# Layer norm, SwiGLU forward and value projection as one written stage; SwiGLU backward in written order; all activations turned by DMA transposes

## The chip, the cores and the metric

One core of one Trainium2 chip. The metric is the device time of one execution in microseconds (us). Each kernel was run several times beside the kernel before on the same chip; all runs that enter a ratio are of the same (fast) state. Most readings below are of stages, because two executions of the same code differ by 10 us and more in the long middle of this program, whatever was changed at its ends (4327 to 4366 us in the fifteen profiles with the change).

Names: PE is TensorE, DVE VectorE, ACT ScalarE, Pool GpSimd and SP SyncE; a DMA queue is called after the engine that issues its transfers. PSUM tiles are the buffers that the matmuls write to. The clock is the share of PE's full clock that was granted, the DMA share the mean busy share of the 16 DMA engines. A turned load is a DMA issued with `dma_start_transpose`: it transposes what it moves (the trace has it as DMA_TRANSPOSE; where the recorded texts say crossbar, they mean these). A hole is a stretch in which PE stands idle.

## The reference, cut to what matters

```python
xn = _layernorm(x)                         # x: 2048 x 640, bf16
s  = recurrent_attention(xn, mem0, Wq, Wk, Wv, Wo)   # 64 segments of 32 rows, 32 heads of 128
h  = silu(xn @ w1) * (xn @ w3)             # 2048 x 1728
g  = silu(h @ w2)                          # 2048 x 640
out = x + s * g
# returned: out, and the gradients of x, mem0, Wq, Wk, Wv, Wo, w1, w3, w2 (jax.vjp)
```

The scans over the segments, forward and backward, are the long middle. The change rewrites what lies in front of them (layer norm, SwiGLU forward, projections of the first rows) and behind them (gradient of Wo, SwiGLU backward, gradients of w1, w3, w2). Some small loads in the scans change their form.

Of the kernel before, what the change touches and what calls it, by code (L numbers as in the profile page):

```python
# [16 lines left out]
P = 128  # L17
# [23 lines left out]
class K:  # L41
# [55 lines left out]
    def setup_consts(self):  # L97
# [9 lines left out]
        self.mean_all = const.tile([P, self.NT], F32, name="mean_all")  # L107
# [44 lines left out]
    def setup_dram(self):  # L152
# [7 lines left out]
        self.XNT = mk("XNT", (D, S))  # L160
        self.SLT = mk("SLT", (F, S))
        self.DUT = mk("DUT", (F, S))
        self.HB = mk("HB", (S, F))
# [3 lines left out]
        self.GST = mk("GST", (D, S))  # L167
# [191 lines left out]

def phase3_Afwd(k, W4, Wv, Wk_):  # L360
# [5 lines left out]
    with tc.tile_pool(name="b0", bufs=1) as io, tc.tile_pool(name="b0s", bufs=3) as stp, \  # L366
            tc.tile_pool(name="b0p", bufs=4, space=bass.MemoryType.PSUM) as ps:
        xs = io.tile([P, DC, k.NB0], BF16, name="b0x")
        nc.sync.dma_start(xs[:], k.XNT[:, 0:k.NB0].rearrange("(dc p) t -> p dc t", p=P))
        wq = k.A_Wq.rearrange("(dc p) h e -> p dc (h e)", p=P)  # L370
        wo = k.A_Wo.rearrange("h e d -> e h d")
        fetch = [(Wq[:, dc], wq[:, dc]) for dc in range(DC)] + [(Wo[:, h:h + 8], wo[:, h:h + 8]) for h in range(0, H, 8)]
        n = 0
        for wi, (W, dst) in enumerate(((Wv, k.QVX[:, 1]), (Wk_, k.KX[:, :]), (Wq, k.QVX[:, 0]))):
            for x0 in range(0, k.NB0, 112):
                for cg in range(4):
                    if n % 3 == 0 and n > 5 and fetch:
                        nc.scalar.dma_start(*fetch.pop(0))
                    n += 1
                    st = stp.tile([112, 1024], BF16, name="b0st", tag="b0st")  # L380
                    for b in range(2):
                        c0 = cg * 1024 + b * 512
                        pb = ps.tile([112, 512], F32, name="b0pb", tag="b0pb")
                        for dc in range(DC):
                            nc.tensor.matmul(pb[:], xs[:, dc, x0:x0 + 112], W[:, dc, c0:c0 + 512],
                                             start=(dc == 0), stop=(dc == DC - 1))
                        k.copy(st[:, b * 512:(b + 1) * 512], pb[:], eng='vs'[b])
                    nc.sync.dma_start(dst[x0:x0 + 112, cg * 1024:(cg + 1) * 1024], st[:])
        assert not fetch

    with tc.tile_pool(name="ast", bufs=1) as st, tc.tile_pool(name="achain", bufs=1) as ch, \
# [22 lines left out]
        def ride_ld(t):  # L414
            x0 = k.NB0 + 24 * t
            b, sub = t // 4, t % 4
            if sub == 0 and x0 < S:
                w = min(96, S - x0)
                rt = ch.tile([P, DC, 96], BF16, name="ride", tag="ride")
                nc.sync.dma_start(rt[:, :, 0:w], k.XNT[:, x0:x0 + w].rearrange("(dc p) s -> p dc s", p=P))  # L420
# [340 lines left out]
def gx_ld(k, xs, x0, eng):  # L761
    w = min(P, k.S - x0)
    eng.dma_start(xs[:, :, 0:w], k.GST[:, x0:x0 + w].rearrange("(dc p) t -> p dc t", p=P))
# [13 lines left out]
def phase3b_out(k, Wo, W0, W4):  # L777
# [12 lines left out]
    with tc.tile_pool(name="oio", bufs=1) as io, tc.tile_pool(name="oac", bufs=1, space=bass.MemoryType.PSUM) as pa, \  # L790
# [59 lines left out]
        def gox_ld(x0):  # L850
            xs = io.tile([P, DC, P], BF16, name="g0x", tag="g0x", bufs=2)
            gx_ld(k, xs, x0, nc.scalar)
# [60 lines left out]
def phase4_Abwd(k, out2, WoT, WvT, WkT, WqT, later):  # L913
# [3 lines left out]
    with tc.tile_pool(name="gst", bufs=1) as st, tc.tile_pool(name="gchain", bufs=1) as ch, \  # L917
# [26 lines left out]
        def ride_ld(t):  # L944
# [3 lines left out]
            if sub == 3:  # L948
                rt = ch.tile([P, DC, 96], BF16, name="gride", tag="gride")
                nc.sync.dma_start(rt[:], k.GST[:, 96 * b:96 * b + 96].rearrange("(dc p) s -> p dc s", p=P))  # L950
# [279 lines left out]
        def gox(x0, cg, b):  # L1230
            if cg == 0 and b == 0:
                uu["gx"] = ch.tile([P, DC, P], BF16, name="gx0", tag="xp", bufs=1)
                gx_ld(k, uu["gx"], x0, nc.gpsimd)
# [263 lines left out]
def phase6b_gWo(k, gow, orr0, out6, gz, late):  # L1497
# [4 lines left out]
    with tc.tile_pool(name="o6", bufs=1) as hp, tc.tile_pool(name="o6i", bufs=2) as io, \  # L1502
# [28 lines left out]
        for qd in range(8):  # L1531
            orr = orrs[qd]
            for jp in range(2):
# [4 lines left out]
                if qd > 1 and late:  # L1538
                    out_, in_ = late.pop(0)
                    if in_ is k.w2:  # L1540
                        turned_load(k, out_, in_)
                    else:
                        nc.scalar.dma_start(out_, in_)
# [8 lines left out]
                for j in range(2):  # L1552
# [4 lines left out]
                    nc.sync.dma_start(out6f[hh * P:(hh + 1) * P, :], ot[:])  # L1557
# [5 lines left out]
def phase1_ln(k: K):  # L1563
    nc, tc = k.nc, k.tc
    D, DC, NT = k.D, k.DC, k.NT
    with tc.tile_pool(name="ln_io", bufs=3) as io, tc.tile_pool(name="ln_sm", bufs=4) as sm, \
            tc.tile_pool(name="ln_ps", bufs=2, space=bass.MemoryType.PSUM) as ps:
        half = D // 2
        assert half <= nc.vector.BN_STATS_FMAX
        for tt in range(NT):  # L1570
            xt = io.tile([P, D], BF16, name="xt", tag="xt")
            k.dma(xt[:], k.A_x[tt * P:(tt + 1) * P, :])
            stats = sm.tile([P, 2, nc.vector.BN_STATS_DIM], F32, name="stats", tag="stats")
            xv = xt[:].rearrange("p (a b) -> p a b", a=2)
            nc.vector.bn_stats(stats[:, 0, :], xv[:, 0, :])
            nc.vector.bn_stats(stats[:, 1, :], xv[:, 1, :])
            mv = sm.tile([P, nc.vector.BN_AGGR_DIM], F32, name="mv", tag="mv")
            nc.vector.bn_aggr(mv[:], stats[:])
            rs = k.rstd_all[:, tt:tt + 1]
            nc.scalar.activation(rs, mv[:, 1:2], ACT.Sqrt, bias=k.eps_t[:], scale=1.0)  # L1580
            nc.vector.reciprocal(rs, rs)
            nc.vector.tensor_copy(k.mean_all[:, tt:tt + 1], mv[:, 0:1])
            nmr = sm.tile([P, 1], F32, name="nmr", tag="nmr")
            nc.vector.tensor_tensor(nmr[:], mv[:, 0:1], rs, ALU.mult)
            nc.vector.tensor_scalar(nmr[:], nmr[:], -1.0, None, op0=ALU.mult)
            xn = io.tile([P, D], BF16, name="xn_t", tag="xn_t")
            nc.vector.tensor_scalar(xn[:], xt[:], rs, nmr[:], op0=ALU.mult, op1=ALU.add)
            k.dma(k.XN[tt * P:(tt + 1) * P, :], xn[:])
            pt = ps.tile([P, DC, P], BF16, name="lnT", tag="lnT")
            for dc in range(DC):  # L1590
                nc.tensor.transpose(pt[:, dc, :], xn[:, dc * P:(dc + 1) * P], k.ident[:])
            xnT = io.tile([P, DC, P], BF16, name="xnT_t", tag="xnT_t")
            k.copy(xnT[:], pt[:])
            k.dma(k.XNT[:, tt * P:(tt + 1) * P].rearrange("(dc p) t -> p dc t", p=P), xnT[:])



def phase2_Bfwd(k: K, Wv, Wk_):
    nc, tc = k.nc, k.tc
    D, DC, S, F, FC = k.D, k.DC, k.S, k.F, k.FC  # L1600
    BLK = 512
    NBLK = S // BLK
    fszs = [min(P, F - fc * P) for fc in range(FC)]
    with tc.tile_pool(name="bw", bufs=1) as wp, tc.tile_pool(name="bio", bufs=2) as io, \
            tc.tile_pool(name="bwork", bufs=2) as wk, \
            tc.tile_pool(name="bps", bufs=2, space=bass.MemoryType.PSUM) as ps, \
            tc.tile_pool(name="bps1", bufs=1, space=bass.MemoryType.PSUM) as ps1:
        w1s = wp.tile([P, DC, F], BF16, name="w1s")
        k.dma(w1s[:], k.w1.rearrange("(dc p) f -> p dc f", p=P))
        w3s = wp.tile([P, DC, F], BF16, name="w3s")  # L1610
        k.dma(w3s[:], k.w3.rearrange("(dc p) f -> p dc f", p=P))
        w2s = wp.tile([P, FC, D], BF16, name="w2s")
        for fc in range(FC):
            k.dma(w2s[:fszs[fc], fc, :], k.w2[fc * P:fc * P + fszs[fc], :])

        nc.gpsimd.dma_start(Wv[:], k.A_Wv.rearrange("(dc p) h e -> p dc (h e)", p=P))
        k.x_rows(k.HRO, k.XN, nc.gpsimd)
        for blk in range(NBLK):
            if blk == 1:
                nc.gpsimd.dma_start(Wk_[:], k.A_Wk.rearrange("(dc p) h e -> p dc (h e)", p=P))  # L1620
            b0 = blk * BLK
            xnT = io.tile([P, DC, BLK], BF16, name="xnT_b", tag="xnT_b")
            nc.scalar.dma_start(xnT[:], k.XNT[:, b0:b0 + BLK].rearrange("(dc p) t -> p dc t", p=P))
            hBT = io.tile([P, FC, BLK], BF16, name="hBT", tag="hBT")
            for fc in range(FC):
                fsz = fszs[fc]
                pg = ps.tile([P, BLK], F32, name="pg", tag="pg")
                pu = ps.tile([P, BLK], F32, name="pu", tag="pu")
                for dc in range(DC):
                    nc.tensor.matmul(pg[:fsz, :], w1s[:, dc, fc * P:fc * P + fsz], xnT[:, dc, :],  # L1630
                                     start=(dc == 0), stop=(dc == DC - 1))
                for dc in range(DC):
                    nc.tensor.matmul(pu[:fsz, :], w3s[:, dc, fc * P:fc * P + fsz], xnT[:, dc, :],
                                     start=(dc == 0), stop=(dc == DC - 1))
                sig = wk.tile([P, BLK], BF16, name="sig", tag="sig")
                nc.scalar.activation(sig[:fsz], pg[:fsz], ACT.Sigmoid)
                sl = wk.tile([P, BLK], BF16, name="sl", tag="sl")
                nc.vector.tensor_tensor(sl[:fsz], pg[:fsz], sig[:fsz], ALU.mult)
                ut = wk.tile([P, BLK], BF16, name="ut", tag="ut")
                nc.scalar.copy(ut[:fsz], pu[:fsz])  # L1640
                nc.vector.tensor_tensor(hBT[:fsz, fc, :], sl[:fsz], ut[:fsz], ALU.mult)

                ds = wk.tile([P, BLK], BF16, name="ds", tag="ds")
                nc.vector.scalar_tensor_tensor(ds[:fsz], sig[:fsz], 1.0, sl[:fsz], op0=ALU.subtract, op1=ALU.mult)
                nc.vector.tensor_tensor(ds[:fsz], sig[:fsz], ds[:fsz], ALU.subtract)
                nc.vector.tensor_tensor(ds[:fsz], ds[:fsz], ut[:fsz], ALU.mult)
# [264 lines left out]
```

## The kernel before: the parts that the change touches

Layer norm is a phase of its own and writes its rows (XN) and their transposes (XNT). Then SwiGLU forward, in blocks of 512 rows, with a scheduler free to order it:

```python
nc.gpsimd.dma_start(Wv[:], ...)                     # 5.2 MB
k.x_rows(k.HRO, k.XN, nc.gpsimd)                    # rows into the scans' layout, DRAM to DRAM, 2.5 MB
for blk in range(4):
    xnT <- XNT (plain load, scalar)
    for fc in range(14):                            # hidden chunks of 128 (the last: 64 rows)
        pg, pu = 5 + 5 matmuls of 512 columns       # w1, w3
        sig (ACT), sl, hBT, ds x3 (DVE), stores of sl and ds on sync
    for ti in range(4):
        pz = 28 matmuls of 320 columns (w2); gb, dz, gs (DVE) and their stores
        5 transposes of gs and 14 of hBT by matmuls with the identity, copied by DVE and ACT
    # ... (cut)
```

SwiGLU backward at the end, in blocks of 256 rows:

```python
for b0 in range(0, S, 256):
    xn_all[...] <- XN                               # gpsimd
    for f0 in range(0, 14, 2):                      # pairs of hidden chunks
        sl, du <- SLT, DUT                          # scalar, three buffers
        pghb = 5 matmuls; ggT = pghb * du; guT = pghb * sl      # DVE
    for ti in range(2):
        pgx = 56 matmuls of 320 columns             # row gradient
        28 transposes of ggT, guT by matmuls, copied by DVE and ACT; store of gu
        norm of the row gradient, o1 = ... (gpsimd), store
```

## Time and profile before

| | us |
|---|---|
| time before, median of 3 runs | 5483.78 (5476.4 to 5496.66) |
| first hidden matmul | 61.7 |
| projections of the first rows over | 492.1 |
| scans and their gradients, to the first matmul of the gradient of Wo | 4339.6 |
| gradient of Wo, of w2 | 175.7, 85.2 |
| SwiGLU backward loop (first hidden matmul to first matmul of the gradient of w1) | 258 |
| gradients of w1, w3 | 117 |

The windows of these stages, from the profile of the kernel before (length, busy time with counts of PE, PE's weight loads, DVE, ACT, POOL; then granted clock, DMA share, GB/s):

```profile
62.00:330.00 268.00, 225.53 (x1313) 116.75 (x1311) 176.28 (x360) 99.78 (x161) 3.12 (x4) 0.92 0.55 189
330.00:492.00 162.00, 159.31 (x720) 94.98 (x720) 49.67 (x72) 41.54 (x71) 0.00 (x0) 0.98 0.49 161
...
5094.00:5352.00 258.00, 238.79 (x1904) 163.36 (x1905) 144.89 (x353) 42.36 (x64) 26.63 (x23) 0.99 0.39 118
```

The projections are full of matmuls; the stage in front of them loses 42 us and some clock; the loop is busy for 239 of 258 us at a clock of 0.99, but 448 of its 1904 matmuls are transposes. Read the DMA share beside them: 0.39 in the loop looks like room.

### The profile page before, as it was taken

What the parts mean: (1) busy time and instruction counts of PE and PEld (TensorE: products, weight loads), DVE (VectorE), ACT (ScalarE), POOL (GpSimd) and SP (SyncE); (2) the same over time, 40 slices, a digit from 0 to 9 for tenths busy, and PEclk for the clock granted to TensorE, in tenths of its full rate; (3) what the DMA queues carried; (4) which work ended last, traced back from release to release, by engine and by line L of the source; (5) the groups of instructions that cost most, each with busy time, mean ns of one, the idle gap of its engine ahead of it and who ended that gap; (6) DMA issues with size and microseconds to landing.
All of it is one profiled execution on the core that took longest, in us unless ns stands there. A gap on an engine that the chain in (4) does not pass through costs nothing. (4 is left out here: it accounts for less than half of the span.)

```text
span 5474.2 us, 163087 instructions
## 1 busy us (share of the span) xinstructions
PE 4830.6 (88%) x66012; PEld 3050.2 (56%) x66012; DVE 2297.2 (42%) x7285; ACT 1752.0 (32%) x4913; POOL 1558.4 (28%) x2673
## 2 busy tenths in 40 slices
PE   4988899989999785999999998789998999999999
PEld 2544555555555443555666665555566555666665
DVE  5833555555555423444444443322233222311451
ACT  2422455555555422232333332222233222301111
POOL 0000334343444212333333332432344333310100
PEclk9998999999999787999999999899999999999999
DMA  7553455555544587666766664744355444657332
GB/s 248 177 188 91 134 154 159 154 159 156 159 154 149 131 190 156 175 185 173 194 182 179 185 184 111 164 113 96 96 134 124 111 106 97 167 178 184 111 111 94
DMA packets 1004358, 822.92 MB, mean 150 GB/s; under 512 B 507009, under 2 KB 892333, under 8 KB 1000929
## 3 DMA queue, kind: packets, MB, share of 16 engines
q1 hardware_dynamic: 758779, 559.22, 37.2%
q0 software_dynamic: 95696, 155.10, 10.3%
q10 hardware_dynamic: 149130, 98.17, 6.5%
q8 instruction: 521, 8.54, 0.7%
q14 instruction: 232, 1.90, 0.1%
HBM read 476.95 MB, written 303.09 MB: 142 GB/s over the span
## 5 line engine op out<-in xcount | busy, mean ns | idle before, releaser
L1411 PE MATMUL wg<-gr,hr 128*128 128x512 bf16 x2400 | 529.4, 382 | 16.1 <-DVE dST L1335 12.9
L1390 PE MATMUL g<-w,ghacc 128*128 128x320 bf16 x3072 | 456.8, 307 | 0.0
L1411 PEld LDWEIGHTS <-hr 128*128 128x128 bf16 x2400 | 235.5, 98 | 301.5 <-issue 27.3
L1390 PEld LDWEIGHTS <-ghacc 128*128 128x128 bf16 x3072 | 301.9, 100 | 120.1
L308 PEld LDWEIGHTS <-hx 128*32 128x32 bf16 x7680 | 180.0, 97 | 170.0 <-issue 13.7
L90 DVE CAST wgo<-wg 128x512 bf16<-128x512 f32 x72 | 47.5, 687 | 524.5 <-issue 268.1
L90 DVE CAST stg<-bank 128x512 bf16<-128x512 f32 x256 | 177.0, 691 | 208.9 <-PE bank L308 197.2
L327 PEld LDWEIGHTS <-gkv 128*8 128x8 bf16 x8192 | 189.8, 87 | 109.1 <-DVE gkv L1002 24.6
L611 ACT ACTIVATE xP<-xsp,xnm 120x120 bf16<-120x120 f32 (+1 forms) x704 | 240.0, 375 | 8.7 <-DVE xnm L607 5.4
L660 POOL DMA_DIRECT2D OR<-xv x163 | 92.7, 569 | 470.5 <-ACT xv L659 347.7
L1154 POOL DMA_DIRECT2D DSR<-gdS x176 | 101.0, 574 | 434.7 <-DVE gdS L1152 410.7
L92 ACT CAST wgo<-wg 128x512 bf16<-128x512 f32 x48 | 25.8, 589 | 572.0 <-PE wg L1411 572.0
L1351 ACT CAST gr<-r6p 120x512 bf16<-120x512 f32 x160 | 93.8, 586 | 357.5 <-PE r6p L1344 255.3
L1223 PE MATMUL gbank<-WqT,ident 128*128 128x512 bf16 x640 | 204.8, 404 | 0.0
L622 POOL TENSOR_TENSOR xP<-xP,xrz 120x480 bf16<-120x480 bf16 x163 | 161.7, 992 | 136.1 <-ACT xP L611 96.1
L1399 DVE TENSOR_TENSOR ghacc<-ghacc,g 128x320 f32<-128x320 f32 x192 | 93.5, 487 | 244.7 <-PE g L1390 244.7
L1152 DVE SCALAR_TENSOR_TENSOR gdS<-gdp,Dx,gPr 120x120 bf16<-120x120 f32 (+1 forms) x680 | 182.8, 330 | 0.0
L245 POOL DMA_DIRECT2D r<-GOS x256 | 144.0, 566 | 130.1 <-PE r6p L1344 92.1
L1359 POOL DMA_DIRECT2D GSP<-grs x48 | 25.6, 539 | 534.6 <-ACT grs L1351 517.4
L308 PE MATMUL gbank<-WoT,gox 128*32 128x512 bf16 x2560 | 153.6, 386 | 24.2 <-POOL gox L957 20.9
L327 PE MATMUL bank<-Wo,oTm 128*32 128x320 bf16 x4032 | 170.2, 320 | 0.1
L1123 POOL DMA_DIRECT2D VTD<-gvT x176 | 130.6, 744 | 137.1 <-ACT gvT L1122 115.8
(342 smaller groups left out, 11150.4 us busy)
## 6 DMA issues: line engine op xcount, KB each, us to landing
QVS<-stg SPq DMA_DIRECT2D x128, 256.0 KB
gqv<-QVS SPq DMA_DIRECT2D x108, 192.0 KB
vTt<-VTD SPq DMA_DIRECT2D x64, 320.0 KB
VTD<-gvT POOLq DMA_DIRECT2D x168, 120.0 KB, 3.6
DSR<-gdS POOLq DMA_DIRECT2D x168, 120.0 KB, 3.5
dS<-DSR SPq DMA_DIRECT2D x168, 120.0 KB
P<-PR SPq DMA_DIRECT2D x168, 120.0 KB
gPr<-PR SPq DMA_DIRECT2D x164, 120.0 KB
```

The lines of the kernel that those rows point to most:

```text
L90: return nc.vector.tensor_copy(out, in_)
L245: eng.dma_start(d, src if src.shape[0] > 1 else src[0])
L308: k.nc.tensor.matmul(bank[32 * g:32 * g + 32, :], x[:, dc, :], W[:, dc, c0:c0 + 512], start=(dc == 0), stop=(dc == k.DC - 1), tile_positio ...
L327: k.nc.tensor.matmul(pm[p0:p0 + nq, 0:320], x[:, h, :], W[:, h, 320 * b:320 * b + 320], start=(first and i == 0), stop=(last and i == 15), ...
L611: nc.scalar.activation(Pb[0:n, j, 0:n], sp[0:n, j, :], ACT.Exp, bias=nmx[0:n, j:j + 1], scale=k.scale, accum_out=Z[0:n, j:j + 1])
L622: eng.tensor_tensor(Pb[0:n, :, 0:n], Pb[0:n, :, 0:n], bc_last(rz[0:n], n), ALU.mult)
L1123: nc.gpsimd.dma_start(k.VTD[tl][:, :, h0:h0 + 4, :], vTq[:])
L1152: nc.vector.scalar_tensor_tensor(dS[0:n, j, 0:n], dp[0:n, j, :], Dx[0:n, j:j + 1], Pr[0:n, j, 0:n], op0=ALU.subtract, op1=ALU.mult)
L1154: nc.gpsimd.dma_start(k.DSR[tl][:, h0:h0 + 4, :], dS[0:n])
L1223: nc.tensor.matmul((bA if g in ("W1", "G1", "G2") else bB)[:], k.ident[:], WqT[:, 0, 0:512], start=True, stop=True)
L1390: nc.tensor.matmul(pg[:], ring[:, i, j, r0:r0 + P], Ws[qd][i][:, j, 320 * h:320 * h + 320], start=(i == 0 and j == 0), stop=(i == 2 and j ...
L1411: nc.tensor.matmul(accs[dc][:], hr[:, tl, dc * P:(dc + 1) * P], grs[i][:, tl, :], start=(tl == 0), stop=(tl == NF - 1))
```

## The change

Its intent: take the transposes off TensorE and let turned loads bring everything that must be turned; start the hidden matmuls early by joining layer norm with SwiGLU forward; put the down projection of a block between the hidden chunks of the next; in the backward loop put the row gradient of a block between the hidden products of the next, so that PE never waits for DVE. Both stages are fixed to their written order on every engine. The core of the diff, with cuts:

```diff
-            nc.gpsimd.dma_start(Wv[:], ...); k.x_rows(k.HRO, k.XN, nc.gpsimd)
+    for blk in range(NBLK):
+        for fc in range(FC):
+            hidden(blk, fc)                      # stores of sl and ds on gpsimd now
+            if blk == 0:  ...                    # layer norm of the later tiles, spread over fc
+                if fc == 9:  fetch(1)            # turned load of the next block's rows (SP)
+                if fc == 12: nc.scalar.dma_start(Wv[:], ...)
+                if fc == 13: k.x_rows(k.HRO, k.XN, nc.sync)
+            elif fc == 0: hidden_out(blk - 1); up_ld(blk - 1, 0); up_ld(blk - 1, 1)   # Gt, scalar, 2 buffers
+            elif fc < 9 and fc % 2 == 0: up(blk - 1, fc // 2 - 1)                     # down projection
+            elif fc == 9: fetch((blk + 1) % NBLK)
+            elif fc == 11 and blk == 1: nc.scalar.dma_start(Wk_[:], ...)
+    # ... (the projection of the first rows with Wv, the last block's up between them)
-                nc.tensor.transpose(pgs..., gs...); nc.tensor.transpose(pht..., hBT...)   # gone
-            nc.sync.dma_start(rt, k.XNT[...])
+            turned_load(k, rt, k.XN[...])        # also gride and gx in the scans, from GS
@@ backward loop
+    for n, (b, i) in enumerate(pairs):
+        ld(n + 3)                                # sl on scalar, du on gpsimd, 4 buffers
+        hid(b, i)                                # products; one turned load of ggT per chunk (SP)
+        next(work, None)                         # a piece of the row gradient of block b - 1
+        if i == FC // 2 - 1:
+            hid_out(b)                           # store of gu, gpsimd, 0.88 MB
+            rows_ld(b)                           # xn_all on gpsimd; gar, ln_G on scalar
+            work = rowgrad(b)                    # calls norm: scr on ACT, o1 and its store on gpsimd
```

## The prediction

> **What bounds the kernel now.** I read the page first: PE is busy 88% of 5474.2 us, and the digits of its row dip at the very start only, so the question is what PE does there and at the end, the two places that the change rewrites. The middle (about 495 to 5007 us) keeps its written order. I then cut the first 500 us and the last 650 us into windows, asked each for its groups, and followed the end by the chain of waits. The windows of the start:
>
> ```profile
> 0.00:20.00 20.00, 0.00 (x0) 0.00 (x0) 1.73 (x9) 0.00 (x0) 3.33 (x22) 1.00 0.93 339
> 20.00:50.00 30.00, 7.63 (x55) 5.09 (x55) 22.61 (x97) 8.16 (x18) 0.00 (x0) 1.00 0.81 229
> 50.00:100.00 50.00, 25.61 (x100) 11.12 (x101) 19.96 (x61) 11.41 (x20) 3.12 (x4) 0.83 0.84 311
> ...
> 150.00:200.00 50.00, 49.84 (x307) 26.36 (x305) 40.67 (x84) 23.93 (x39) 0.00 (x0) 1.00 0.54 173
> ```
>
> The columns are length, then busy time of PE, PE's weight loads, DVE, ACT, POOL, then granted clock, DMA share, GB/s. For 20 us nothing computes while 339 GB/s of weights arrive ahead of the inputs; from 20 to 50 us the layer norm is DVE's; from 50 to 100 us PE waits half the time at a clock of 0.83. From 150 us on PE is full. The groups of the first 560 us say with what:
>
> ```profile
> L1638 DVE TENSOR_TENSOR sl<-pg,sig 128x512 bf16<-128x512 f32 (+1 forms) x56 | 38.3, 684 | 19.5 <-DMA SLT<-sl 13.8 <-ACT sig L1636 4.1 <-ACT ut L1640 0.8
> L1644 DVE SCALAR_TENSOR_TENSOR ds<-sig,sl 128x512 bf16<-128x512 bf16 (+1 forms) x56 | 38.2, 683 | 17.6 <-DMA DUT<-ds 17.5
> L1646 DVE TENSOR_TENSOR ds<-ds,ut 128x512 bf16<-128x512 bf16 (+1 forms) x56 | 23.5, 419 | 0.9
> L1682 PE MATMUL pht<-ident,hBT 128*128 128x128 bf16 x224 | 16.8, 218 | 2.1 <-ACT hb_tok L1686 2.1
> ```
>
> The SLT and DUT rows are early stalls behind stores (31 us of DVE), which PE feels; pht is a transpose by identity matmuls that the change drops. The windows of the end, then the chain of waits there:
>
> ```profile
> 4829.00:5010.00 181.00, 177.57 (x1299) 127.28 (x1300) 30.22 (x67) 12.92 (x34) 25.46 (x48) 0.99 0.73 229
> 5010.00:5040.00 30.00, 17.23 (x151) 12.38 (x149) 3.44 (x7) 4.56 (x7) 1.43 (x2) 0.85 1.08 205
> 5040.00:5100.00 60.00, 59.04 (x410) 37.48 (x408) 11.13 (x28) 5.02 (x13) 4.23 (x6) 0.99 0.18 54
> 5100.00:5350.00 250.00, 233.01 (x1857) 158.79 (x1856) 138.44 (x334) 40.85 (x61) 22.39 (x18) 0.99 0.38 116
> ```
>
> ```profile
> 4831.70 175.31 PE oa L1550 x1277
> ...
> 5017.54 17.78 DMA x<-in_B_w_dram
> ```
>
> So the gradient of Wo is a solid matmul stretch, 175.31/1277 = 0.137 us each at 320 columns. Then PE loses about 20 us behind the turned w1 and w3 loads: the turns of gz share their tile and ACT sits behind them. The SwiGLU backward loop (first matmul 5094.5, last transpose copied at 5352.7, so 258 us) is PE-full, but with what? The timeline of PE in one block:
>
> ```profile
> 5186.68 2.18 PE L1775 MATMUL pgxb<-x,ggT 128*128 128x320 bf16 x14
> 5188.79 2.18 PE L1775 MATMUL pgxb<-x,guT 128*128 128x320 bf16 x14
> 5190.90 1.03 PE L1782 MATMUL ptt<-ident,ggT 128*128 128x128 bf16 x14
> 5191.87 1.03 PE L1782 MATMUL ptt<-ident,guT 128*128 128x128 bf16 x14
> ```
>
> Fourteen row-gradient matmuls start 2.11 us apart as a group, where 14 x 0.137 = 1.92: the last has only 64 rows and costs 0.19 us extra. Fourteen transposes take 0.96 us.
>
> [...] clock 0.83 in the window with gaps, 1.00 in full ones, so filling gaps pays twice. [...] w1 and w3 (4.26 MB) were issued from 5007.4 and let the chain go at 5035.3, so 153 GB/s, with the DMA share at 1.08. I use 153. [...]
>
> **The change, part by part.**
>
> *Forward.* Before, the first hidden matmul is at 61.7 us in PE's timeline and the last matmul of the first-rows projections at 492.1. After:
> - Start. Four input tiles come first on the queue, not behind 4.4 MB of weights. I choose 6 us to land, 5 for four tiles' statistics, 3 for rstd and rows, 4 for the stores and 5 for the crossbar to bring them back: first matmul near 23 us.
> - Block 0. DVE per hidden chunk: 0.684 + 4 x 0.418 = 2.36 us (the 683 ns scalar form becomes a 417 ns tensor_tensor, ACT makes 1 - sigmoid for another 0.6). 14 x 2.36 = 33, plus layer norm of 12 tiles at 0.49 + 0.47 + 0.20 + 0.44 = 1.6 us: 19, sum 52. These tiles' loads stand behind 3.1 MB of w1 and w3, and DVE runs in order: 7 us of waiting. Ends near 82 (before: 123).
> - Blocks 1 to 3. PE: 140 hidden matmuls x 0.2165 (240 in 51.96 us in the projection) = 30.3, plus 112 down matmuls x 0.137 = 15.3, sum 45.6, without transposes and 64-row matmuls. DVE: 33 + 4 x (0.824 + 3 x 0.483) = 42.1. PE bound; in the chunks without a down projection DVE's 2.36 beats PE's 2.17, so I take 47 (before: 54.4 from 120.8 to 284.1). Ends near 223.
> - Last down projections with the Wv rows: 52 + 15.3 = 67, plus 6 where DVE's in-order work delays PSUM copies: 296.
> - Wk and Wq rows: 104, plus 4 for the turned load and 4 because the Wq and Wo fetches are 1.5 times denser: 408. Saved: 492 - 408 = 84.
>
> *Gradient of Wo.* Same matmuls, 175 us. hb now comes by four crossbar loads of 1.77 MB.
>
> *Gradient of w2.* 448 x 0.139 = 62 us after 5008, against 5093.5 - 5008.1 = 85.4: 23 saved. The 16 turns of gz (2.6 MB, 17 us at 153 GB/s) follow w1 and w3 on SP, done near 5055, 15 us before they are used.
>
> *Loop.* Per block of 256 rows PE keeps 70 x 0.11 (five take 0.55 in the timeline) = 7.7 and 112 x 0.137 = 15.3: 23.0 us, against 31.1 now. The difference is 56 transposes (3.9), eight 64-row matmuls (1.5), and about 2.6 of waits for sl loads, PSUM and copies. DVE: 28 x 0.417 + 2 x 3.36 = 18.4, below PE. Block 0 has no row gradient beside it and is DVE's, 12 us; then 7 x 23.3; then the last row gradient, 15.3. Sum 190 against 258: 68 saved.
>
> *Gradients of w1, w3.* 117 us as before. The crossbar load of gu (7.1 MB at 153 GB/s = 46 us, from about 5 us in) hides behind the first 58.6 us half. The final store moves to Pool's queue, about +1 us.
>
> Sum: 84 + 23 + 68 - 1 = 174; I take off 2 for the 28 small turned loads in the scans, whose issue on SP (1.2 us at the least among turned loads) is longer than a plain one's 0.4. 5484 - 172 = **5312 us**.
>
> **The rivals.**
> 1. *Crossbar traffic becomes the bound.* In the Wo stage the share is 0.73 already. Per 22 us step: operand rows 8 us of all engines, row tiles 3, outputs 2, turned hb 1.77 MB at 153 to 186 GB/s 10 to 12: 23 to 25. For: this exceeds the step. Against: operand rows are fetched a step ahead and precede hb in the same queue, and two steps without hb follow, so only hb itself slips, unneeded until 5008. If wrong, PE starves 10 to 30 us and the total is near 5330.
> 2. *SP's issue or DVE is the loop's bound.* 14 turns per block at about 1 us of SP issue is 14 of 23 us; Pool's loads of du queue behind its 1.4 us additions and the large gu store. For: three pairs of prefetch is 9.8 us only. Against: four PSUM buffers carry two pairs. At 26 us per block the loop takes 209, the total 5331.
> 3. *The gain at the start is not had.* Block 0 waits for inputs behind weights, table loads between Sigmoid and Sqrt stall ACT (1.28 us each, six of them). With block 0 ending at 100 instead of 82, total 5330. That DVE bounds blocks 1 to 3 would make them 50: +9.
>
> Two of these at once give about 5350. The other side: DVE starts overlap their neighbours' ends by some 0.07 us, and the waits that I chose (7, 6, 4, 4) may not show: 5290.
>
> **Range and chances.** 5280 to 5360 holds it 8 times in 10. 2% is 110 us, so faster by over 2% needs under 5374: all three rivals at once would be just past it. Faster 0.94, same 0.05, slower 0.01.
>
> **What would show it.** Right: first hidden matmul near 23 us; projections over by about 408; no PE matmul that reads the identity in the two stages; w2 gradient 62 us without a hole; loop blocks 23 to 24 us with PE full at clock 0.99; gap between gradient halves none. Wrong: holes in the Wo stage released by the operand load, PE waiting for DVE products released by du or sl loads, gaps in the second half waiting for gutok, or the middle moved by more than 10 us.

## The result

The changed kernel took 5410.48 us (median of 4 runs, 5397.13 to 5420.56) against 5480.2 of the kernel before in the same rounds. A ratio here is the mean time of one kernel's fast runs over that of the other's of the same rounds, so not quite the ratio of the medians quoted: 0.9866, interval 0.9835 to 0.9896. That is 1.3% faster ("same" by the 2% mark that the record's verdicts use), where 3.1% was predicted (172 of 5484 us); the time lies above the predicted range of 5280 to 5360.

The same windows in the profile of the changed kernel:

```profile
24.00:324.00 300.00, 253.17 (x1248) 133.21 (x1248) 192.53 (x419) 131.16 (x233) 99.66 (x180) 0.94 0.64 200
324.00:441.00 117.00, 106.93 (x480) 63.38 (x480) 33.16 (x48) 28.36 (x49) 0.00 (x0) 0.97 0.63 192
...
5031.00:5269.00 238.00, 199.94 (x1457) 146.87 (x1457) 125.02 (x316) 12.45 (x31) 95.91 (x134) 0.93 0.72 161
```

The transposes are gone (1457 matmuls in the loop), but PE now stands idle for 38 of 238 us there and runs at a clock of 0.93. Before, it was idle for 19 of 258, at 0.99. The stages, from the two profiled runs (span 5474.2 before, 5395.4 after):

| stage | before | predicted | after |
|---|---|---|---|
| first hidden matmul at | 61.7 | 23 | 24.0 |
| forward blocks 0 to 3, by their first hidden matmul (block 3 to the end of its last) | 63.9, 59.7, 53.6, 47.5 | 59, 47, 47, 47 | 52.4, 67.2, 53.9, 48.4 |
| all projections over at | 492.1 | 408 | 440.4 |
| middle, to the gradient of Wo | 4339.6 | +2 | 4345.6 |
| gradient of Wo | 175.7 | 175 | 175.7 |
| gradient of w2 | 85.2 | 62 | 67.3 |
| backward loop | 258 | 190 | 238 |
| gradients of w1, w3 | 117.0 | 117 | 119.9 |

Where did it go? First the forward stage, block 1. The waits in its window of the changed kernel, then its timeline (start, length, engine, line, operation; in brackets the idle time before and what ended it):

```profile
PE pg L1625 <- DVE sl L1634: 15.6, 2, 14.3
DVE gs L1670 <- DMA Gt<-in_grad_out_dram: 13.9, 1, 13.9
```

```profile
108.63 0.49 DVE L1670 TENSOR_TENSOR gs<-Gt,gb 128x640 bf16<-128x640 bf16 x1 [13.95 <-DMA Gt<-in_grad_out_dram]
...
111.45 2.29 PE L1625 MATMUL pg<-xnT_b,w1s 128*128 128x512 bf16 x5 [14.30 <-DVE sl L1634]
```

DVE, fixed to its written order, stands for 14 us in front of a load of 160 KB; nothing that it writes for PE gets past that place, and PE runs dry. Note also the length of PE's first five matmuls after the gap: 2.29 us, where five take 1.24 otherwise. The clock was granted at half from 100.3 to 117.4 us. And it is not that all DMA engines are full: the DMA share from 94 to 106 us is only 0.39.

Then the loop. Pool's, DVE's and PE's timelines at the start of one block:

```profile
5106.27 1.40 POOL L1892 TENSOR_TENSOR o<-gxn,ln_G 128x640 bf16<-128x640 f32 x1 [4.85 <-DVE gxn L1890]
5107.96 0.57 POOL L1893 DMA_DIRECT2D out_dram<-o  x1 [0.30 <-POOL o L1892]
5108.53 1.17 POOL L1855 DMA_DIRECT2D GU<-guT  x1
5110.26 0.75 POOL L1823 DMA_DIRECT2D xn_all<-XN  x1
5111.01 0.72 POOL L1816 DMA_DIRECT2D du<-DUT  x1
...
5119.04 0.42 DVE L1848 TENSOR_TENSOR ggT<-pghb,du 128x256 bf16<-128x256 f32 x1 [8.88 <-DMA du<-DUT]
...
5119.85 2.29 PE L1846 MATMUL pghb<-x,w2T 128*128 128x256 bf16 x10 [3.96 <-DVE guT L1849]
```

Read it from the bottom. PE waits for DVE, DVE waits 8.88 us for a du load, and that load was issued at 5111.01, behind the o1 addition (which waited for DVE's norm), the store of gu and the load of xn_all, and landed 8 us later. DVE had used its last loaded pair at 5110. The like happens in each of the last six of the eight blocks (7.8 to 9.4 us each, 2.9 in the second block): 56.8 us of DVE waits for du in the loop.

### The profile page after: what moved, and what is told of

The parts are those of the page before. It is cut to its first block, busy times and chain, and to the rows that moved or that the text cites. A ratio compares the mean times of both kernels' runs of the same rounds, so it can differ in the third digit from the quotient of the medians.

```text
span 5395.4 us, 161274 instructions
## 1 busy us (share of the span) xinstructions
PE 4754.1 (88%) x65100; PEld 3008.7 (56%) x65100; DVE 2251.5 (42%) x7164; ACT 1727.6 (32%) x4899; POOL 1747.9 (32%) x3001
## 5 line engine op out<-in xcount | busy, mean ns | idle before, releaser
L90 DVE CAST wgo<-wg 128x512 bf16<-128x512 f32 x72 | 47.5, 687 | 528.3 <-issue 271.1
L324 PEld LDWEIGHTS <-gkv 128*8 128x8 bf16 x8192 | 189.2, 87 | 117.8 <-DVE gkv L1009 22.5
L336 DVE TENSOR_TENSOR fsum<-gbank,fup 64x160 bf16<-64x160 f32 x128 | 40.5, 317 | 313.4 <-ACT fup L335 313.4
```

Source lines behind the costliest of these rows:

```text
L90: return nc.vector.tensor_copy(out, in_)
L324: k.nc.tensor.matmul(pm[p0:p0 + nq, 0:320], x[:, h, :], W[:, h, 320 * b:320 * b + 320], start=(first and i == 0), stop=(last and i == 15), ...
```

## The experiments

Two figures are followed: when the projections are over (changed kernel 440.4; in the six other runs that leave the forward stage as changed, 442 to 445), and the length of the loop (changed kernel 237.8; in the runs that leave the loop as changed, 239 to 242). Block 1 is read here from the first matmul of its first down projection to the same of block 2: 66.6 us as changed, and 66.8 to 71.1 in the six other runs. Of all the totals, only those of e14 and e15 are "faster" by the 2% mark; e11 is "unclear", e6, e7 and c1 are single runs of unknown state, and the rest are "same": gains of some 10 us are read from the stages. Each edit is against the changed kernel unless it says otherwise.

### Forward: what holds Gt?

**e1_hro_halfrows** splits the row copy into halves of a row:

```diff
-        eng.dma_start(A[...][:, 0:96], X[...])
+        for h in range(2):
+            c = slice(320 * h, 320 * h + 320)
+            eng.dma_start(A[...][:, 0:96, c], X[...][:, :, c])
```

> The changed kernel, with the copy of the normalized rows into the scans' layout (HRO<-XN, DRAM to DRAM) split into two column halves, so that it moves 640-byte rows and no longer 61,440-byte packets; queue, place and bytes stay. Theory F1 (in block 1 of the forward stage the loads of Gt, 1,280-byte packets on ACT's queue, take turns with 61 KB packets of this copy and so take 14 us): DVE's gs then waits under 4 us for Gt in block 1, PE's gap of 14.3 us near 111 us goes, block 1 goes from 67.1 to 48 to 53 us, total 10 to 20 us less than the changed kernel (about 5395). Rival F2 (Gt stands behind the 5.2 MB of Wv in the same queue): block 1 stays at 65 to 69. Rival F3 (DVE is itself the bound): the wait for Gt shrinks, but block 1 stays above 60.

Measured: 5405.99 us, ratio 0.9871 (0.9838 to 0.9904). Block 1 took 51.2 us, PE's gap is gone, the projections were over at 430.0. F1 held for the stage. The total shows little of it: in this run's profile the middle was 18 us longer than in the first (see below). In the trace of the changed kernel the copy ran in packets of 61,440 bytes, 2.3 us each, and of the loads in packets of 1,280 bytes on ACT's queue only 41 got through between 94 and 106 us, against 121 in the next 3 us; 28 of the large ones began in those 12 us. The packets of that trace alternate: from 95 to 103 us the large ones begin in rounds of seven, 2.5 us apart, and ahead of each round begin seven packets of ACT's queue (0.06 us each) and seven of 4,096 bytes of Pool's (0.16 us). Turn for turn, the small ones lose.

One side effect shows in SP's timeline of this run:

```profile
86.10 19.59 SPq L252 DMA_DIRECT2D HRO<-XN  x2
105.73 12.50 SPq L254 DMA_DIRECT2D HRO<-XN  x1
118.33 33.48 SPq L271 DMA_TRANSPOSE xnT_b<-XN  x4
```

With small packets SP is busy issuing for 32 us (1.5 us with large ones), and the next block's turned load comes after it. The large ones are not free for SP either: in the changed kernel the turned load behind them took 18.9 us to issue, from 87.7 to 106.6 us.

**e2_wv_on_pool**:

```diff
-                        nc.scalar.dma_start(Wv[:], ...)      # and Wk_
+                        nc.gpsimd.dma_start(Wv[:], ...)
```

> The changed kernel with the loads of Wv and Wk put on Pool's queue (as in the kernel before) in place of ACT's; the row copy stays as changed. Theory F2 (Gt waits because it stands behind Wv in ACT's queue): the wait of gs for Gt in block 1 falls from 14 us to under 4, block 1 from 67.1 to 48 to 53 us. Theory F1 (the 61 KB packets of the row copy starve Gt's small ones): block 1 keeps 60 us or more, with Gt still over 8 us, and the stores on Pool's queue (sl, ds, gb) may come to wait behind Wv, which would make DVE wait for SLT and DUT stores again as in the kernel before.

Measured: 5436.47 us, ratio 0.9929. Block 1 took 73.9 us, the projections were over at 454.4. Gt came in time now, but a store took its place:

```profile
DVE sl L1634 <- DMA SLT<-sl: 24.5, 1, 24.5
```

F2 is right in that Gt no longer waits, and useless: the bulk load and the row copy only stand in front of another small transfer. The stage is worse for it. With e1 and e9 it shows that Gt's wait took both: Wv ahead of it on its queue (Gt was issued at 78.8, 7 us before the copy), and the row copy beside it once its turn came. With one of the two out of the way it did not wait.

**e9_rows_at_end** moves the row copy, whole rows, to a place without Gt:

```diff
-                    if fc == 13:
-                        k.x_rows(k.HRO, k.XN, nc.sync)
+            if n == 12:                        # among the projections with Wv
+                k.x_rows(k.HRO, k.XN, nc.sync)
```

> The changed kernel with the row copy HRO<-XN, whole rows and on SP as changed, but issued among the projections of Wv, after the last down projection, in place of the end of block 0; nothing else moves. Theory F1 (this copy beside the load of Gt is what holds DVE and PE in block 1): the 14 us wait of gs for Gt and PE's 14 us gap go, block 1 falls from 67 to 50 to 54 us, the Wv rows are over 10 to 18 us earlier (306 to 314 us, 323.7 as changed). If only the small packets of half rows helped in the first experiment, by slowing the copy, block 1 is as short here. Rival F2 (Gt stands behind Wv in ACT's queue): block 1 keeps 62 us or more.

Measured: 5409.96 us, ratio 0.9867. Block 1 took 53.5 us: F1 held again, with no help from small packets. But the projections were over at 441.4, no gain, because the copy did the same to its new neighbours. The waits around 300 us:

```profile
DVE b0st L90 <- DMA QVX<-b0st: 10.8, 1, 10.8
```

The small stores of the projected rows now ran beside the large packets, and PE had a hole of 9.0 us. So this transfer is not hidden anywhere as it is; it chooses its victim.

**e6_rows_and_dz** and **e7_rows_and_gt4** both keep the half rows; the first writes ACT's second sigmoid ahead of DVE's product, the second gives Gt four buffers:

```diff
+            dz = ...; nc.scalar.activation(halves(dz), pz..., ACT.Sigmoid, scale=-1.0)   # e6: moved up
             gb = ...; nc.vector.tensor_tensor(halves(gb), pz..., halves(sz), ALU.mult)
-            dz = ...; nc.scalar.activation(...)
```

```diff
-            Gt = wk.tile([P, D], BF16, name="Gt", tag="Gt")              # e7
+            Gt = wk.tile([P, D], BF16, name="Gt", tag="Gt", bufs=4)      # all four loaded at the block's start
```

> The changed kernel with the row copy in half rows (as in the first of these experiments, which gave a forward stage 10.4 us shorter) and, in the down projection, the second sigmoid (dz) written ahead of DVE's product gb. Theory G1 (ACT's dz waits for gb because it is written after it, then DVE waits 0.77 us for dz, twelve times in blocks 1 to 3, and this makes block 2 last 54 us in place of 47): the idle 0.77 before DVE's dz goes, block 2 falls to 48 to 50. Rival G2 (the load of Gt, issued by ACT in written order, waits for its buffer until DVE's gs is done and so holds ACT's next sigmoids): block 2 stays at 53 to 55.

> The changed kernel with the row copy in half rows and four buffers of Gt in place of two, all four loads issued at a block's start, so that none waits for a buffer. Theory G2 (ACT stands at the issue of Gt until DVE's gs is done): the waits of ACT's sig for DVE's gs (4.30 and 1.92 us in two steps of block 2) go, block 2 falls from 54 to 48 to 50 us, and the Wv rows, where the last block's down projections run, shrink from 77.7 to about 73. Rival G1 (order of dz): the small waits of DVE for dz stay and block 2 stays at 53 to 55.

Measured: 5408.0 and 5407.91 us (one run each, state unknown). In both, blocks 2 and 3 took 46.7 and 43 us (as changed 52.2 and 45.5, all by their down projections), so by themselves they look like two proofs. They are none: both had a new hole of 31.8 and 17.1 us ahead of block 2 (from 128 and 129 us), in which Wk landed (130 to 160 and 130 to 150 us; as changed 140 to 160, beside block 2), so that its load was no longer beside that block. They do not tell G1 from G2. What e7 does show, beyond the hole, is the last part of the stage: from the first of the last block's down projections to the end of the Wv rows 70.5 us against 74.3 as changed and 73.8 in e6; in the six other runs with the changed forward stage it took 72.6 to 74.3. That is G2, for 2 to 4 us.

**e8_all_mends** put e6, e7 and the mend of the loop (below) together.

> The changed kernel with the row copy in half rows, four buffers of Gt, dz ahead of gb and loads seven pairs ahead. If F1, G1 or G2, and T4 hold together: forward stage over by 415 to 422 us (440 as changed), loop 200 to 212 us (238), total 5345 to 5375, so a ratio to the kernel before of 0.976 to 0.982. If the gains are lost later (rows arriving earlier but the scans taking longer) the forward stage is over early and the total stays above 5390.

Measured: 5417.51 us, ratio 0.9911 (0.9891 to 0.9931): no better than the changed kernel, if anything worse. The groups of PE from 120 to 180 us name the reason:

```profile
L1627 PE MATMUL pg<-xnT_b,w1s 128*128 128x512 bf16 (+1 forms) x26 | 7.6, 425 | 47.5 <-DMA xnT_b<-XN 47.4
```

The turned load of 0.66 MB for block 2 was held back behind SP's long issue of half rows, then ran beside the 5.2 MB of Wk, and landed 52 us after SP had begun to issue it. The expected gain did not vanish: it moved PE forward into a collision.

**e10_front_spread** takes the collisions apart: row copy at the end, Gt in four buffers and loaded a block early, Wv and Wk in blocks 1 and 2 behind the turned loads.

```diff
-                    if fc == 12: nc.scalar.dma_start(Wv[:], ...)      # block 0
-                elif fc == 11 and blk == 1: nc.scalar.dma_start(Wk_[:], ...)
+                elif fc == 12 and blk == 1: nc.scalar.dma_start(Wv[:], ...)
+                elif fc == 12 and blk == 2: nc.scalar.dma_start(Wk_[:], ...)
+                if fc == 10:
+                    for ti in range(TB): up_ld(blk, ti)
```

> The row copy at the end as in the run above; Gt in four buffers and loaded in the block before its use; the loads of Wv and Wk one block later each (blocks 1 and 2), so that neither stands ahead of a Gt that is waited for, nor beside a block's turned load that is about to be used. If F1 and G2 hold together and the 32 and 47 us holes of the two mended kernels before (PE waiting for the turned xnT_b beside Wk) were a collision of the turned load with the 5.2 MB of Wk: no hole over 3 us between 30 and 300 us, blocks 1 to 3 at 46 to 50 us each, Wv rows over by 292 to 300 us, Wq rows by 410 to 417. Rival (the turned load itself is slow, whatever lies beside it): a hole of 10 us or more stays at a block's start.

Measured: 5413.2 us, ratio 0.9868. Blocks 1 to 3 took 47.9, 50.7 and 47.6 us, no hole at a block's start; a hole of 9.1 us stayed at the row copy's new place, as in e9; projections over at 428.8. A turned load is not slow by itself, then. Whether Wk beside it or its lateness behind SP's issue made the 47 us was not separated: both were taken away together.

### Loop: what holds du?

**e3_du_on_act**:

```diff
-                        for (t_, src, q) in ((sl, k.SLT, nc.scalar), (du, k.DUT, nc.gpsimd)):
+                        for (t_, src, q) in ((sl, k.SLT, nc.scalar), (du, k.DUT, nc.scalar)):
```

> The changed kernel with the loads of du in the SwiGLU backward loop on ACT's queue in place of Pool's; nothing else moves. Theory T1 (du stands on Pool's queue behind the o1 addition and the store of gu, so that DVE's product ggT waits some 8.8 us in each block): the waits of ggT for DUT fall from 56.8 us to under 10, the loop from 238 to 195 to 210 us, the total 28 to 43 us below the changed kernel. Rival T2 (the turned loads of ggT and the DMA share of 0.73 slow every load): du still lands late from the other queue, waits of 30 us or more, loop above 225. Rival T3 (loads on ACT's queue are held by ACT's own waits, scr above all): waits move to sl and du together, loop 225 to 245.

Measured: 5428.79 us, ratio 0.9916; loop 245.5 us. T1, as I had it, fell. The waits of this run:

```profile
ACT scr L1885 <- DMA ggtok<-ggT: 68.0, 4, 17.5
...
DVE ggT L1848 <- DMA du<-DUT: 39.2, 12, 6.9
PE pghb L1846 <- DVE guT L1849: 39.2, 13, 7.0
```

Fewer us of waiting for du, in more places, and PE no better. ACT's queue is no free lane: its loads stand in program order behind the scr activation, which waits for the norm, behind the load of ln_G, whose buffer is free only after o1 on Pool, and, in the trace, at semaphores last signalled by SP's turned loads of ggT (the 68.0 us in four waits above). That is T3; which of these holds the queue longest was not separated.

**e4_no_gg_turns** (w1's gradient wrong on purpose, all else correct):

```diff
-                            turned_load(k, ggtok[...], ggT[0:fsz, fc, :])
+                nc.gpsimd.memset(ggtok[:], 0.0)       # once, before the loop
```

> The changed kernel without the 112 turned loads of ggT in the loop; ggtok is filled with zeros once, so the gradient of w1 is wrong on purpose. Theory T1 (order on Pool's queue): the loop gains little, 238 to 222 to 238 us, because du still stands behind the store of gu; the waits for DUT stay above 35 us. Rival T2 (crossbar traffic slows the other loads): the waits for DUT fall below 15 us and the loop comes to 195 to 210.

Measured: 5420.73 us; loop 246.8 us, of which 22.5 are one hole at the memset (my edit's own cost), so 224 without it. DVE still waited 69.7 us for du (22 of them that hole). So without a single turned load the loop is 13 us shorter, and DVE's waits for du, without that hole, are 47 us against 57. T2 is out as the main cause.

**e5_seven_ahead**:

```diff
-                        sl = bp.tile(..., tag="sl5", bufs=4); du = bp.tile(..., tag="du5", bufs=4)
-                        ld(n + 3)
+                        sl = bp.tile(..., tag="sl5", bufs=8); du = bp.tile(..., tag="du5", bufs=8)
+                        ld(n + 7)
```

> The changed kernel with the loads of sl and du in the SwiGLU backward loop seven pairs ahead (eight buffers each) in place of three (four buffers); queues and order of everything else stay. Theory T4, formed after the runs before (moving du to ACT's queue gave nothing: the loop stayed at 245 us; so both queues are held, Pool's by the o1 addition and the stores, ACT's by the scr activation and the load of ln_G that waits for o1, for some 12 us at each block's end, and a load then takes 8 us more, against a lead of three pairs): waits of ggT for DUT fall from 56.8 us to under 10, the loop from 238 to 200 to 212 us. Rival T5 (the loop is held by the chain of the norm on DVE and by PSUM, not by the loads): waits for DUT go but the loop stays above 225 with DVE idle for other reasons. Rival T2b (the DMA engines are full, so earlier loads only queue earlier): waits for DUT stay above 30 us.

Measured: 5406.36 us, ratio 0.9897 (0.9877 to 0.9916); loop 226.3 us. All waits for du went, and only 11 us came of it. The waits that stand there now:

```profile
DVE scr L1887 <- DMA xn_all<-XN: 29.2, 7, 6.4
PE pghb L1846 <- DVE guT L1849: 24.5, 7, 9.0
```

One wait had hidden the next. DVE now reaches the norm early and waits for xn_all, which stands on Pool's queue behind the 0.88 MB store of gu.

**e13_xn_early_three_ahead** mends that one alone; **e11_xn_early** mends both:

```diff
                         hid(b, i)
+                        if i == 3:
+                            xn_ld(b)          # load of xn_all, taken out of rows_ld
```

> The loop with the load of xn_all issued in the middle of its block, ahead of the store of gu, and nothing else: sl and du stay three pairs ahead. If the place of xn_all alone was the cost (it held Pool's queue, and with it du): loop 199 to 206 us, as with seven ahead. If the lead was a cost by itself (du behind o1 and the store of gu): waits for DUT of 30 us or more stay, loop 222 to 236 us.

> The loop with loads of sl and du seven pairs ahead and the load of xn_all issued in the middle of its block, ahead of the store of gu (in the run with seven ahead the loop took 226 us and DVE waited 29.2 us for xn_all in seven waits, and ACT's loads stood for turned loads of ggT). Theory T6 (the xn_all load behind the store of gu is what is left): waits for xn_all go, loop 203 to 212 us. Rival T3 (ACT's loads wait at their issue for the completion of turned loads that share a DMA semaphore): waits for xn_all go, but loads of gar and sl still come late and the loop stays above 218.

Measured: e13 5402.01 us, ratio 0.9852, loop 227.7; e11 5385.12 us, ratio 0.9811 (0.9781 to 0.9842), loop 199.0. The wait that decides in each; of e13:

```profile
DVE ggT L1850 <- DMA du<-DUT: 46.8, 7, 8.3
```

and of e11:

```profile
PE pghb L1848 <- DVE guT L1851: 10.6, 2, 9.2
```

Either mend alone is worth 10 or 11 us, both together 39. The two waits lie one behind the other on the same path, so taking one away only lets the path run into the other. In e11 four of the last five blocks take 23.1 us each (by their first ggT), with the clock full from 5099.7 to the end. What is left is one hole of 9.2 us in the second block, the first with a row gradient in it. There DVE waits 7.2 us for gar, one of ACT's first loads, which by the trace's releasers stand behind turned loads (ACT's scr waits 31.6 us once for ggtok).

**e12_loads_on_pool** is e11 with sl, gar and ln_G on Pool's queue as well:

> As the run above, with the loads of sl, gar and ln_G on Pool's queue too, so that ACT issues no load in the loop. Theory T3 (semaphores shared between ACT's loads and SP's turned loads hold ACT): ACT's waits for turned loads go, DVE's and PE's gaps at the block starts go, loop 195 to 206 us. Rival T6 (xn_all alone was left): the same as the run above within 3 us. Rival T7 (Pool's in-order queue with the o1 addition in it holds its now 16 more loads): waits for SLT appear on DVE, loop above 220.

Measured: 5416.14 us, ratio 0.9874; loop 209.9. The hole in the second block went (0.4 us), so it is ACT's queue that makes it, as T3 has it; shared semaphores by themselves were not tested. But DVE now waited 33.6 us for gar, in eight waits, and the gradient of w2 ahead of the loop grew to 84.0 us (71.2 in e11), with a hole of 11 us. T7 in kind, though for gar and not for sl: Pool's queue cannot take the load.

### The middle, and the sum

**c1_before_again** is the kernel before:

> The kernel before, unchanged, for a second profile. From the first matmul after the hole at the projections' end to the first matmul of the gradient of Wo it took 4324.5 us in its one profile; the thirteen profiles with the change took 4327 to 4366, mean 4346. If the difference of 20 belongs to the spread of all kernels: this profile shows 4335 us or more. If it belongs to the change: 4318 to 4332.

Measured: 5473.85 us (one run). Measured from behind the 15 us gap at the projections' end (so 15 less than in the table), its middle took 4321.8 us, so 4322 to 4325 in two profiles of the kernel before, against 4345 in the mean of fifteen with the change (4327 to 4366). Both lie below all fifteen. So the difference of 22 us is put down to the change, though no single run tells it from the spread.

**e14_spread_and_early** joins the mends without the collisions: e10's front, but with the row copy in half rows behind the last turned load of block rows; dz ahead of gb; e11's loop.

```diff
+                elif fc == 10 and blk == 2:
+                    k.x_rows(k.HRO, k.XN, nc.sync)      # half rows
```

> All mends, with the two collisions taken out: row copy in half rows after the last fetch of turned rows (block 2), Gt in four buffers a block early, Wv and Wk in blocks 1 and 2, dz ahead of gb, sl and du seven pairs ahead, xn_all in the middle of its block. If they add up: Wq rows over by 412 to 420 us, loop 196 to 202, total 5335 to 5365, ratio to the kernel before 0.974 to 0.980. If the half rows' long issue on SP holds the turned load of the last block: a hole of 10 us or more near 225 us and Wq rows over at 425 or later.

Measured: 5351.58 us (5344.86 to 5357.06), ratio 0.9755 (0.9732 to 0.9778). This kernel is correct and beats both. Its windows:

```profile
24.00:299.00 275.00, 247.78 (x1231) 132.08 (x1248) 192.07 (x419) 131.18 (x232) 99.60 (x180) 0.97 0.66 218
299.00:416.00 117.00, 107.51 (x482) 63.31 (x480) 33.00 (x48) 28.45 (x49) 0.00 (x0) 0.97 0.62 193
...
5034.00:5232.00 198.00, 188.44 (x1458) 142.48 (x1459) 125.62 (x316) 12.64 (x31) 92.56 (x129) 0.97 0.90 189
```

Against the changed kernel: the same work of every engine, 25 us less in the forward stage (projections over at 415.5) and 40 less in the loop (197.5). The DMA share in the loop is 0.90 now, up from 0.72: the same bytes in less time. One load is still late: in the second block DVE waits 5.4 us for gar, and PE has a hole of 7.9 us, most of what the loop still takes over 190.

**e15_plain_scan_loads** is e14 with the small turned loads of the scans as plain loads of the same bytes (data wrong on purpose):

```diff
-                turned_load(k, rt[:, :, 0:w], k.XN[x0:x0 + w, :])            # ride; so too gride, gx
+                nc.sync.dma_start(rt[:, :, 0:w], k.XN[...].rearrange("s d -> (s d)").rearrange("(p c s) -> p c s", p=P, c=DC))
```

> The kernel of the run above with the 28 small turned loads in the scans (ride, gride and gx) replaced by plain loads of the same bytes from the same tensors, on the queues of the kernel before: the data in them are wrong on purpose. If these turned loads cost the middle of the program its 18 us: the middle takes 4318 to 4335 us and the total falls by 10 to 20 us against the run above. If it is spread: the middle stays within 4327 to 4366, in particular the stretch of the backward scans where gx is loaded late (8 us longer in all thirteen profiles) is the only one that shrinks, by 5 to 8 us.

Measured: 5336.39 us (5329.43 to 5351.06), ratio 0.9730; middle 4340.8, against 4354.5 in e14. The total fell by the 15 us expected of the cause, but the middle not to the range given. (The profiled run was the slowest of its five, 5351.06 us against 5329 to 5338 for the others, so its readings may be on the long side.) One part is shown, in the backward scans around the loads of gx, which the change had moved from Pool's and ACT's queues to SP. There the changed kernel waits

```profile
PE gbank L778 <- DMA gx<-GS: 13.2, 1, 13.2
```

where the kernel before had

```profile
PE gbank L771 <- DMA gx<-GST: 5.6, 1, 5.6
```

In all fifteen profiles with the change this wait is 12.7 to 13.9 us; in e15 the matmul does not wait there, only its weight load does, for 5.0 us. (A second wait for gx, 17 to 23 us, is in every kernel, e15 too.) So 7 to 8 us of the middle belong to the way gx is loaded (turned, and on SP; e15 takes back both at once). The rest stays open: between some 820 and 1270 us into the middle the kernels with the change take some 11 us longer than the first profile of the kernel before, and e15 does too, but c1, the same kernel as that, took 8 us longer there as well.

## Why the prediction was wrong, point by point

- **Start, and block 0.** Right, and better than chosen: first hidden matmul at 24.0, block 1 began at 76.4 where 82 was predicted. The 7 us of waiting for late tiles did not show (DVE waited 1.7 us for one). Rival 3's block 0 did not come.
- **"Blocks 1 to 3 ... I take 47."** This step failed, for 20 us in block 1 and 7 in block 2. I counted PE and DVE work, which was nearly right (block 3 took 48.4; e10 and e14 have 47 to 51 for all three), and no transfer at all. The row copy had been in the kernel before too, and the diff shows that it moved to SP, at the end of block 0: just where Gt is loaded for the first time. That e1 and e9 each took block 1 to 51 and 53 us shows the cause; that e2 freed Gt too shows that Wv ahead of it on ACT's queue was needed as well. Most of block 2's 7 us is not settled; Wk beside it is the suspect.
- **Wv, Wk and Wq rows.** 77.7 for 73, a gap of 7.1 for 4, and 109.6 for 108. Small terms, each a little mis-sized. With four buffers of Gt the first is smaller (73.8 in e7). Forward in all: 32 us less than the 84 predicted.
- **Gradient of Wo, and rival 1.** Right. 175.7 us, at a DMA share of 0.96: the turned loads did not starve it.
- **Gradients of w2, and of w1 and w3.** 67.3 for 62, and 119.9 for 117 (117.0 in e11 and e14). The hole behind the turned weights went as predicted; two short waits for PSUM copies and stretched matmuls remain. (The transposes that the change took off TensorE were short in a row: fourteen took 0.96 us in the kernel before.)
- **Loop, "then 7 x 23.3".** This step failed most: 29.4 us a block, 238 for 190. The work was sized right, since e11 and e14 show 23.1. What failed is the sentence in rival 2, "four PSUM buffers carry two pairs". I had the suspects there (du behind the additions and the gu store, 9.8 us of lead) and let PSUM settle it. PSUM let PE run ahead of DVE (to 5115.9 us in the block shown, where DVE had stopped at 5110.2); it did not bring du to DVE. The measured chain is 12 us of late issue and 8 us of landing against a lead of some 10. And I had not seen the second wait behind it, xn_all behind the gu store. Each of PE's idle stretches of 3.2 to 4.9 us ended in 3.4 to 6.8 us at half clock, which I had used in the other direction only ("filling gaps pays twice").
- **"I take off 2 for the 28 small turned loads".** Mis-sized: the middle is 22 us longer in the mean, 6 in the first profile. The later gx is 7 to 8 of it; e15 returns 14 in its one profile; the rest stays open. PE's row of digits, which the prediction reads as dipping "at the very start only", has a 7, an 8 and a 5 from about 1916 to 2327 us, where the loads of gx lie.
- **The sum.** In the profiled pair 93 of 172 us are missing: 32 forward, 57 behind the scans (48 of them the loop), 4 in the middle. e14 has 119 of the 172 by its profile, whose run was the slowest of its four (by the ratio of the runs it is 2.45%, some 134 us); of the rest, in that profile, 28 are its middle, 9 the gradient of w2 and 7 or 8 each the forward stage and the loop.
- **The chances.** 0.94 for over 2% rested on rivals of 20 to 25 us each. Rival 2 had nearly the right place and rival 3 the right stage, but not the cause or the block; both had about half the size, because I took for each wait only its first cause.

## What to carry to other kernels

Count a written order's transfers like its instructions: for each load ask what stands ahead of it on its queue, when that can be issued at the latest, and what it shares the DMA engines with, then compare the sum with the lead in buffers. Move small loads that someone is about to use away from bulk copies in large packets (the load of Gt held DVE for 14 us), and put bulk weights behind, not beside, the turned load of the next block (the hole of 47 us in e8 was gone in e10). When one wait is taken away and little comes of it, look for the next wait on the same path before giving up the idea: here two mends were worth 10 us each alone and 39 together.

## What the traces showed of transfers and of small matmuls

- The turned w1 and w3 came at 153 GB/s (kernel before, at a DMA share of 1.08, with some stores and loads beside them), and the turned 0.66 MB of one block, issued beside 5.2 MB of a plain load, took 52 us (e8; how much of that is the neighbour's was not separated).
- Beside a DRAM-to-DRAM copy in packets of 61,440 bytes (2.3 us each), and behind Wv on its queue, a load of 160 KB in packets of 1,280 bytes held DVE for 14 us (changed kernel).
- Splitting such a copy had a price: SP's issue of the same 2.5 MB took 32 us in rows of 640 bytes (e1; 37 us in e8), 1.5 us in large packets (changed kernel), though then the next issue stood 18.9 us.
- A matmul with 64 rows among those of 128 cost 0.19 us extra in the kernel before.
